# The value products of two heads, issued in turn over two PSUM banks

## The chip, the cores and the metric

One Trainium2 chip; the kernel runs on one of its cores. The metric is the device time of one execution in microseconds. TensorE is called PE (its weight loads PEld), VectorE DVE, ScalarE ACT, GpSimd POOL, and SyncE, which here only issues transfers, SP.

## What is computed

Masked attention for 8 batches of 8 heads over 576 positions with 64 values each, then a two-layer block on the 4608 tokens. Heads 0 to 3 of a batch ("plain") see the last 32 positions, heads 4 to 7 ("dilated") every fourth of the last 128.

```python
scores = np.matmul(q, k.transpose(0, 1, 3, 2)) / np.sqrt(D)
scores = np.where(masks[None], scores, -1e9)
attn = np.exp(scores - scores.max(-1, keepdims=True))
attn = attn / (attn.sum(-1, keepdims=True) + 1e-09)
x = np.matmul(attn, v).transpose(0, 2, 1, 3).reshape(B * S, H * D)
h = x @ w_in                        # (4608 x 512) @ (512 x 2048)
g = np.where(h >= 1, h, np.where(h <= -1, 0.0, (h + 1) ** 2 / 4))
return g @ w_out                    # (4608 x 2048) @ (2048 x 512)
```

## The kernel before

**Attention.** A head's 576 queries are cut into six tiles of 96, each of which sees 128 keys. The positions of dilated heads are sorted by their remainder modulo 4 on the host, so that they too have a band of keys. Heads are numbered through, n = 8 x batch + head, and are handled in pairs (n, n + 1). Scores of a head come in three parts of two tiles (`scores_split`, L230; the first 16 heads use `scores_pair`, L207). DVE adds the mask and takes the row maximum (L249, L181), ACT takes the exponential (L255), POOL divides by the sum (L291, the tile `c`), and the result is turned key by query into `pt`: by six DVE transposes (L306) for heads from 16 on, on PE (L330) with a copy out (L333) before that. Even heads use `pt0`, odd heads `pt1`.

**Values.** `values(n)` (L354) multiplies `pt` of the two heads with their values: 64 columns of weights, 96 columns moving, six tiles per head. Head n writes partitions 0 to 63, head n + 1 partitions 64 to 127 of the same PSUM tile. There are two such tiles: part 0 holds query tiles 0 to 2, part 1 tiles 3 to 5. They are called o{n}_0 and o{n}_1. Each fp32 matmul is two records in the trace, so a block has 24. `store_x` copies a tile out as a rounded part `xh` (ACT, L349) and the remainder `xl` (DVE, L350), which the first layer reads. The copies are cut where a block of 512 tokens ends (`cuts`), so a PSUM tile has one or two pieces; those of a dilated pair have two pieces each in the steady stretch, of 32 to 256 columns, since its columns are spread over the whole batch.

**PSUM.** The tag `att` has two banks, shared by the values, the scores from head 10 on, and the PE transposes of head 0 and from head 8 on. A tile that asks for a bank waits for the last reader of the tile that had it.

**The two layers.** 9 tiles of 512 tokens times 16 slices of the hidden width make 144 steps. A step has 12 matmuls of the first layer (L403, in three rounded products), the activation (DVE L417, ACT L420, DVE L422, ACT L423, DVE L426; the tiles y, h, gh, gl), and 12 matmuls of the second layer (L439) two steps later.

**Order.** PE and SP issue in the order of the code; the instructions of DVE, ACT and POOL are ordered by a scheduler that simulates the program. Attention for later batches is put into slots: slot 2s comes behind the first layer of step s, slot 2s + 1 behind its second layer. From head 16 on, for the pair n:

```python
for j, at in ((0, u), (1, u + 4)):
    place(at, lambda m=n + j: scores_split(m, 0))
    place(at + 1, lambda m=n + j: scores_split(m, 2))
    place(at + 2, lambda m=n + j: (scores_split(m, 4), after(m)))
place(u + 11, lambda n=n: values(n))
```

with u growing by 8 from pair to pair. So the slot ahead of values(n) holds the last scores of head n + 2, and the slot behind it the first scores of head n + 3, with 12 matmuls of the second layer between. The DVE transposes of head n + 2 fall behind values(n), too.

Of the kernel before, what the change touches and what calls it, by code (L numbers as in the profile page):

```python
# [22 lines left out]
F32 = mybir.dt.float32  # L23
# [9 lines left out]
QT, NQ = 96, 6  # L33
# [11 lines left out]
def body(ctx, tc, q, k, q2, k2, v, mask, eye, w_in, w_out, out):  # L45
# [5 lines left out]
    ps = ctx.enter_context(tc.tile_pool(name="ps", bufs=1, space=bass.MemoryType.PSUM))  # L51
# [269 lines left out]
    def pt_of(n):  # L321
        return first_pts[n] if n < len(first_pts) else pts[n % 2]
# [23 lines left out]
    def store_x(src, t, c, dst):  # L346
        xh, xl = xtile(t)
        with tc.high_priority(offset=60):
            last["act"] = nc.scalar.copy(out=dst(xh[:, c]), in_=src)  # L349
            last["dve"] = nc.vector.tensor_tensor(  # L350
                out=dst(xl[:, c]), in0=src, in1=dst(xh[:, c]).bitcast(F32), op=ALU.subtract
            )

    def values(n):  # L354

        b, h = divmod(n, H)
        plain = h < H // 2
        c, tok0 = h // 2, b * S

        end = TOK - tok0 % TOK  # L360
        for part in range(2):
            op = ps.tile([128, 512], F32, tag="att", name=f"o{n}_{part}", bufs=2)
            for j in range(2):
                for i in range(3):
                    PE.matmul(  # L365
                        out=op[64 * j : 64 * j + 64, i * QT : (i + 1) * QT],
                        lhsT=heads[n + j]["vt"][:, 3 * part + i],
                        rhs=pt_of(n + j)[:, 3 * part + i],
                        start=True,
                        stop=True,  # L370
                    )
            if plain:
                first = part * 3 * QT
                cuts = sorted({first, min(max(end, first), first + 3 * QT), first + 3 * QT})
                for a, z in zip(cuts, cuts[1:]):
                    t, at = divmod(tok0 + a, TOK)
                    store_x(op[:, a - first : z - first], t, c, lambda x: x[:, at : at + z - a])
            else:
                cuts = sorted({0, min(end // DIL, CLS), CLS})
                for a, z in zip(cuts, cuts[1:]):  # L380
                    t, at = divmod(tok0 + DIL * a, TOK)
                    store_x(
                        op[:, : 2 * CLS].rearrange("p (r i) -> p r i", r=2)[:, :, a:z],
                        t,
                        c,
                        lambda x: x[:, at : at + DIL * (z - a)].rearrange("p (i r) -> p r i", r=DIL)[
                            :, 2 * part : 2 * part + 2
                        ],
                    )
# [89 lines left out]
    def values_native(n):  # L479
        values(n)  # L480
        if n + 2 < native:
            load_values(n + 2)
# [8 lines left out]
    for n in range(native, nhead, 2):  # L491
        u = 27 + 4 * (n - native)
# [4 lines that stand above are left out]
        place(u + 4, lambda n=n: (transpose(n), load_values(n)))  # L497
        place(u + 8, lambda n=n: transpose(n + 1))
        place(u + 11, lambda n=n: values(n))
# [40 lines left out]
    def early_values(n):  # L540
        with tc.high_priority(offset=150):
            values(n)
# [7 lines left out]
    def marks():  # L550
        return last["act"], last["dve"]
# [5 lines left out]
    with tc.manual_schedule(engines={mybir.EngineType.PE, mybir.EngineType.SP}):  # L557
# [19 lines left out]
        first = marks()  # L577
# [110 lines left out]
```

## Time and profile before

| | |
|---|---|
| time, median of 3 runs | 943.05 us (942.95 to 943.52) |
| the profiled execution | 943.52 us, its span 941.7 us |
| granted PE clock, mean | 0.994 |
| PE busy | 924.8 us, 98% of the span |
| DVE, ACT, POOL busy | 685.0, 486.9, 239.8 us |
| values matmuls (L365) | 768 records, 24 to a block |
| steady stretch | one pair of heads every 25.13 us or so, with 24 values records |

Times of single instructions are read from a list in order of time: start, duration, engine, line, tiles (written <- read), partitions x elements, count, and in brackets how long the engine sat idle before it and what ended that. Records of PE overlap, since matmuls are pipelined: the distance of starts is what one costs. In the table of stretches, PEclk is the share of PE's clock that was granted.

### The profile page before, as it was taken

The numbers are of one execution on the slowest core, as the hardware profiler recorded it, in microseconds if no ns is written. First come the engines' busy times: TensorE is split into PE (matmuls) and PEld (weight loads), VectorE is DVE, ScalarE is ACT, GpSimd is POOL, SyncE is SP. The second block draws the span as 40 slices with busy tenths as digits, with TensorE's granted clock in tenths as the row PEclk, the third lists the DMA queues.
The fourth block names the chain that finished last, engine by engine and source line by source line (L and its number), as shares of the span: only waits on it lengthen the run. The fifth ranks groups of instructions, "written<-read, shape, count | busy, mean of one in ns | idle before, by whom it ended". The sixth has DMA issues, their size and how long they took to land.

```text
span 941.7 us, 14427 instructions
## 1 busy us (share of the span) xinstructions
PE 924.8 (98%) x4886; PEld 753.1 (80%) x4886; DVE 685.0 (73%) x1982; ACT 486.9 (52%) x1336; POOL 239.8 (25%) x155
## 2 busy tenths in 40 slices
PE   7989989999999999999999999999999999999998
PEld 6777778888888888888888888888888888888886
DVE  6898877888887888878887888888877643334333
ACT  6778856555555556555555555555555322222222
POOL 4566543222222222222222222222222000000000
PEclk9989999999999999999999999999999999999999
DMA  9971002312232222122322213222321010001001
GB/s 348 406 293 45 1 26 63 106 58 69 69 114 69 69 66 89 57 68 69 114 69 69 64 58 105 69 69 70 113 70 42 2 45 1 1 1 46 0 1 46
DMA packets 31018, 73.87 MB, mean 78 GB/s; under 512 B 3520, under 2 KB 3808, under 8 KB 30944
## 3 DMA queue, kind: packets, MB, share of 16 engines
q1 hardware_dynamic: 30944, 72.94, 23.5%
q8 instruction: 39, 0.64, 0.3%
q14 instruction: 35, 0.29, 0.1%
HBM read 63.49 MB, written 9.44 MB: 77 GB/s over the span
## 4 chain that ended last, share of the span: by engine, by line
PE 89%; DMA 5%; DVE 3%; issue 1%; POOL 1%; ACT 0%; SPq 0%; DVEq 0%; POOLq 0%; ACTq 0%
PE acc L439 41%; PE h L403 40%; PE o L365 4%; PE s L230 4%; DMA wo_raw<-w_in 3%; DMA wi_raw<-w_in 1%; DVE wo_raw L123 1%; DMA vt<-v_in 1%; DVE wo_m L126 1%; DMA kr<-k_in 1%; DVE c L181 1%; POOL c L291 0%; PE t L330 0%; DVE wi_m L126 0%; DVE y L417 0%
## 5 line engine op out<-in xcount | busy, mean ns | idle before, releaser
L439 PE MATMUL acc<-wo,gh 128*128 128x512 f32 x1152 | 385.2, 396 | 0.0
L403 PE MATMUL h<-xh,wi 128*128 128x512 f32 x1152 | 362.3, 396 | 0.8 <-DVE gl L426 0.8
L439 PEld LDWEIGHTS acc<-wo,gh 128*128 128x128 f32 x1152 | 217.0, 188 | 48.4
L403 PEld LDWEIGHTS h<-xh,wi 128*128 128x128 f32 x1152 | 210.1, 189 | 42.8 <-DVE gl L426 1.0
L403 PE MATMUL h<-xl,wi 128*128 128x512 f32 x576 | 227.5, 395 | 0.0
L439 PE MATMUL acc<-wo,gl 128*128 128x512 f32 x576 | 225.6, 392 | 0.0
L143 POOL TENSOR_TENSOR kk<-kr,kk 128x608 fp32r<-128x608 f32 x48 | 94.8, 1976 | 422.3 <-ACT kk L139 422.3
L255 ACT ACTIVATE c<-c 96x128 f32<-96x128 f32 x330 | 129.0, 392 | 118.4 <-DVE c L181 118.4
L420 ACT ACTIVATE y<-y,consts 128x512 f32<-128x512 f32 x144 | 104.1, 723 | 124.9 <-DVE y L417 124.9
L423 ACT CAST gh<-h 128x512 fp32r<-128x512 f32 x144 | 84.4, 586 | 130.4 <-PE acc L439 128.2
L417 DVE TENSOR_SCALAR y<-h 128x512 f32<-128x512 f32 x144 | 99.2, 689 | 62.9 <-PE h L403 61.7
L422 DVE TENSOR_TENSOR h<-h,y 128x512 f32<-128x512 f32 x144 | 100.6, 698 | 49.6 <-ACT y L420 48.2
L403 PEld LDWEIGHTS h<-xl,wi 128*128 128x128 f32 x576 | 108.6, 188 | 25.3
L439 PEld LDWEIGHTS acc<-wo,gl 128*128 128x128 f32 x576 | 108.6, 188 | 21.3
L426 DVE TENSOR_TENSOR gl<-h,gh 128x512 fp32r<-128x512 f32 x144 | 98.5, 684 | 37.2 <-ACT gh L423 37.2
L306 DVE STREAM_TRANSPOSE pt<-c 32x192 f32<-32x192 f32 x288 | 106.0, 368 | 5.8
L249 DVE TENSOR_TENSOR c<-s,msk 96x256 f32<-96x256 f32 (+1 forms) x168 | 61.5, 377 | 39.7 <-PE s L230 38.7
L291 POOL TENSOR_TENSOR c<-c 96x768 f32<-96x768 f32 x56 | 83.0, 1483 | 17.0 <-DVE c L290 16.7
L181 DVE CUSTOM_DVE_ANT_0 c<-s,c 96x128 f32<-96x128 f32 x288 | 70.6, 280 | 1.0
L349 ACT CAST xh<-o 128x288 fp32r<-128x288 f32 (+8 forms) x112 | 38.3, 380 | 46.2 <-PE o L365 30.8
L255 ACT ACTIVATION_READ_ACCUMULATOR c<-c 96x1 f32 x330 | 62.1, 188 | 0.0
L230 PEld LDWEIGHTS s<-kk,qs 128*96 128x96 f32 x288 | 46.4, 161 | 15.7
(57 smaller groups left out, 660.6 us busy)
## 6 DMA issues: line engine op xcount, KB each, us to landing
kr<-k_in SPq DMA_DIRECT2D x56, 304.0 KB, 3.3
qr<-q_in SPq DMA_DIRECT2D x56, 288.0 KB, 2.8
vt<-v_in SPq DMA_DIRECT2D x32, 384.0 KB, 4.0
out<-out SPq DMA_DIRECT2D x36, 256.0 KB, 2.9
wi_raw<-w_in SPq DMA_DIRECT2D x16, 512.0 KB, 9.3
wo_raw<-w_in SPq DMA_DIRECT2D x16, 512.0 KB, 9.4
msk<-mask_in SPq DMA_DIRECT2D x1, 144.0 KB, 3.8
ident<-eye_in SPq DMA_DIRECT2D x1, 36.0 KB, 4.8
```

The lines of the kernel that those rows point to most:

```text
L143: nc.gpsimd.tensor_tensor(out=kk[:, 1], in0=hd["kr"], in1=kk[:, 0].bitcast(F32), op=ALU.subtract)
L230: PE.matmul(out=sv[:, t - t0], lhsT=hd["qs"][:, t * QT : (t + 1) * QT], rhs=hd["ks"][:, :, t * QT : t * QT + 128], start=True, stop=True,)
L255: last["act"] = nc.scalar.activation(out=c[:, t], in_=c[:, t], func=AF.Exp, bias=st[:, 0, t : t + 1], scale=-1.0, accum_out=st[:, 1, t : t ...
L291: nc.gpsimd.tensor_tensor(out=c, in0=c, in1=spread(st[:, 2]), op=ALU.mult)
L306: nc.vector.transpose(out=pt[r : r + 32, :, 32 * g : 32 * g + 32], in_=c[32 * g : 32 * g + 32, :, r : r + 32],)
L403: PE.matmul(out=hp, lhsT=wi[f][:, w, 128 * c : 128 * c + 128], rhs=x[:, c], start=c == 0 and i == 0, stop=c == NC - 1 and i == len(terms) - 1,
L417: nc.vector.tensor_scalar(out=y, in0=hp, scalar1=-1.0, scalar2=1.0, op0=ALU.max, op1=ALU.min)
L420: nc.scalar.activation(out=y, in_=y, func=AF.Square, bias=half_t, scale=0.5)
L422: activated = nc.vector.tensor_tensor(out=hp, in0=hp, in1=y, op=ALU.max)
L423: copied = nc.scalar.copy(out=gh, in_=hp)
L426: nc.vector.tensor_tensor(out=gl, in0=hp, in1=gh.bitcast(F32), op=ALU.subtract)
L439: PE.matmul(out=acc[m], lhsT=g[:, r], rhs=wo[f][:, w], start=f == 0 and i == 0, stop=f == NF - 1 and i == len(terms) - 1,)
```

## The change

Both PSUM tiles of a values block are now taken at its start. The twelve matmuls alternate between the heads. In the first round head n goes through its tiles 0 to 2 into the first bank, while head n + 1 goes through its tiles 3 to 5 into the second; in the second round they swap. The copies out of both tiles follow behind all twelve matmuls, in the same code as before. No matmul, copy or size is changed, and lines behind it move down by three (L365 is L367, L417 is L420, L439 is L442).

```diff
-        for part in range(2):
-            op = ps.tile([128, 512], F32, tag="att", name=f"o{n}_{part}", bufs=2)
-            for j in range(2):
-                for i in range(3):
+        ops = [ps.tile([128, 512], F32, tag="att", name=f"o{n}_{part}", bufs=2) for part in range(2)]
+
+        for first in range(2):
+            for i in range(3):
+                for j in range(2):
+                    part = first ^ j
                     PE.matmul(
-                        out=op[64 * j : 64 * j + 64, i * QT : (i + 1) * QT],
+                        out=ops[part][64 * j : 64 * j + 64, i * QT : (i + 1) * QT],
                         lhsT=heads[n + j]["vt"][:, 3 * part + i],
                         rhs=pt_of(n + j)[:, 3 * part + i],
                         start=True,
                         stop=True,
                     )
+        for part, op in enumerate(ops):
             if plain:
```

## The prediction

> **What bounds the kernel now.** I read the page first: shares of busy time, and the chain that ended last.
>
> ```profile
> PE 924.8 (98%) x4886; PEld 753.1 (80%) x4886; DVE 685.0 (73%) x1982; ACT 486.9 (52%) x1336; POOL 239.8 (25%) x155
> PE acc L439 41%; PE h L403 40%; PE o L365 4%; PE s L230 4%; DMA wo_raw<-w_in 3%; DMA wi_raw<-w_in 1%; DVE wo_raw L123 1%; DMA vt<-v_in 1%; DVE wo_m L126 1%; DMA kr<-k_in 1%; DVE c L181 1%; POOL c L291 0%; PE t L330 0%; DVE wi_m L126 0%; DVE y L417 0%
> ```
>
> PE sets the time; the edited matmuls (L365) are 4% of the chain. Next, busy time by stage, and the groups of PE.
>
> ```profile
> 0.00:60.00 60.00, 51.94 (x440) 44.05 (x441) 48.58 (x219) 44.95 (x127) 32.99 (x28) 0.97 0.99 379
> 200.00:754.00 554.00, 554.00 (x2907) 451.43 (x2907) 448.81 (x1372) 303.56 (x910) 145.95 (x86) 1.00 0.24 72
> L230 PE MATMUL s<-kk,qs 128*96 128x256 f32 x288 | 57.7, 283 | 0.0
> ```
>
> The columns are the stage's length, then busy PE, PEld, DVE, ACT, POOL, granted clock. From 200 to 754 us PE never rests, and the scores (L230) never wait. Whatever lengthens or shortens PE's work there, or makes it wait, moves the end one for one. The first 60 us are held by DMA (0.99 busy), so the four values blocks there (n = 0 to 6) count for nothing.
>
> Then one values block in the steady stretch, n = 36, in order of time (start, duration).
>
> ```profile
> 424.27 0.40 PE L403 MATMUL h<-xl,wi 128*128 128x512 f32 x1
> 424.59 1.43 PE L365 MATMUL o<-pt,vt 128*64 128x96 f32 x24
> 425.95 0.50 PE L439 MATMUL acc<-wo,gh 128*128 128x512 f32 x1
> ...
> 428.58 0.39 PE L439 MATMUL acc<-wo,gh 128*128 128x512 f32 x1
> 428.81 0.40 PE L230 MATMUL s<-kk,qs 128*96 128x256 f32 x2
> 429.05 0.62 PE L403 MATMUL h<-xh,wi 128*128 128x512 f32 x2
> ```
>
> The block (24 records, two to a matmul) is followed by twelve L439 matmuls, and then s39_0, the first scores of head 39.
>
> **Part one: the block itself.** On PE the change puts the heads' matmuls in turn. Here pt0 is head 36, pt1 head 37; o36_0 and o36_1 are the two banks.
>
> Before, on PE at values(36):
>
> ```order
> L403 MATMUL h3_11_4389<-xl3_1952,wi11_1184 128x512
> L365 MATMUL o36_0_4410<-pt0_67,vt36_4211 64x96 x3
> L365 MATMUL o36_0_4410<-pt1_68,vt36_4211 64x96 x3
> L365 MATMUL o36_1_4421<-pt0_67,vt36_4211 64x96 x3
> L365 MATMUL o36_1_4421<-pt1_68,vt36_4211 64x96 x3
> ```
>
> After, the same place (the first eight of twelve):
>
> ```order
> L367 MATMUL o36_0_4410<-pt0_67,vt36_4211 64x96
> L367 MATMUL o36_1_4411<-pt1_68,vt36_4211 64x96
> L367 MATMUL o36_0_4410<-pt0_67,vt36_4211 64x96
> L367 MATMUL o36_1_4411<-pt1_68,vt36_4211 64x96
> L367 MATMUL o36_0_4410<-pt0_67,vt36_4211 64x96
> L367 MATMUL o36_1_4411<-pt1_68,vt36_4211 64x96
> L367 MATMUL o36_1_4411<-pt0_67,vt36_4211 64x96
> L367 MATMUL o36_0_4410<-pt1_68,vt36_4211 64x96
> ```
>
> The heads now alternate without a break, and both banks fill until the end of the block. Do heads overlap on PE? The block n = 2 tells them apart by their buffers (pts_xh, pts_xl):
>
> ```profile
> 23.34 0.71 PE L365 MATMUL o<-pts_xh,vt 128*64 128x96 f32 x6
> ...
> 24.97 0.25 PE L365 MATMUL o<-pts_xh,vt 128*64 128x96 f32 x1
> 24.99 0.25 PE L365 MATMUL o<-pts_xl,vt 128*64 128x96 f32 x1
> 25.05 0.25 PE L365 MATMUL o<-pts_xh,vt 128*64 128x96 f32 x1
> 25.07 0.25 PE L365 MATMUL o<-pts_xl,vt 128*64 128x96 f32 x1
> ```
>
> Each head starts a record every 0.08 us, the other head's between them: they run side by side already, in one and the same bank. What is lost is the lead of the first head. Six records of one head take 0.71, so the last starts 0.71 - 0.25 = 0.46 after the first; twelve would take 0.46 + 6 x 0.083 = 0.96. The block above has its last start at 1.43 - 0.25 = 1.18. If both heads start together, it saves 1.18 - 0.96 = 0.22 us. That instructions in turn do start together is seen at the scores L207, where two heads alternate over two banks:
>
> ```profile
> 109.63 1.12 PE L207 MATMUL s<-kr,qr 64*96 64x128 f32 x16
> ```
>
> Sixteen records of 128 columns in 1.12 are 0.07 each, though one alone should take 0.083 x 128/96 = 0.11: pairs run at once. The bounds are 0 (no better overlap) and 0.22; I take 0.22, since turns give overlap in both rows. The other bank itself gains nothing. The second matmul of a block now needs its bank half a block sooner; its last reader is DVE's reduce of s38_4, which stands ahead of the L140 row at 423.43 below and so is done a microsecond before the block; nothing waits.
>
> **Part two: who reads the banks, and when.** The last matmul now writes o_0, so both banks finish at the block's end, and the scheduler orders the copies out of them (L349 on ACT, L350 on DVE) anew. On DVE behind the block, before:
>
> ```order
> L417 TENSOR_SCALAR y3_11_4402<-h3_11_4389 128x512
> L350 TENSOR_TENSOR xl4_2946<-o36_0_4410,xh4_2945 128x2x64
> L422 TENSOR_TENSOR h3_11_4389<-h3_11_4389,y3_11_4402 128x512
> L350 TENSOR_TENSOR xl4_2946<-o36_1_4421,xh4_2945 128x2x64
> L350 TENSOR_TENSOR xl5_3931<-o36_0_4410,xh5_3930 128x2x80
> L306 STREAM_TRANSPOSE pt0_67<-c38_4317 32x6x32 x6
> L350 TENSOR_TENSOR xl5_3931<-o36_1_4421,xh5_3930 128x2x80
> L249 TENSOR_TENSOR c39_4444<-s39_0_4445,msk_64 96x256
> ```
>
> After:
>
> ```order
> L420 TENSOR_SCALAR y3_11_4402<-h3_11_4389 128x512
> L425 TENSOR_TENSOR h3_11_4389<-h3_11_4389,y3_11_4402 128x512
> L350 TENSOR_TENSOR xl4_2946<-o36_1_4411,xh4_2945 128x2x64
> L350 TENSOR_TENSOR xl4_2946<-o36_0_4410,xh4_2945 128x2x64
> L306 STREAM_TRANSPOSE pt0_67<-c38_4317 32x6x32 x6
> L350 TENSOR_TENSOR xl5_3938<-o36_1_4411,xh5_3937 128x2x80
> L350 TENSOR_TENSOR xl5_3938<-o36_0_4410,xh5_3937 128x2x80
> L429 TENSOR_TENSOR gl3_11_4404<-h3_11_4389,gh3_11_4403 128x512
> L249 TENSOR_TENSOR c39_4444<-s39_0_4445,msk_64 96x256
> ```
>
> Before, one bank (o36_0) was read to its end ahead of the six transposes. Now **both** second pieces stand behind them. s39_0 takes one of these banks: in the built program it waits for the second piece of o36_0 before the change, for that of o36_1 after it. All of PE's queue stands behind s39_0. The same holds for every dilated pair of the steady stretch but the last: n = 20, 22, 28, 30, 36, 38, 44, 46, 52, 54, 60, eleven in all. In plain pairs the next scores wait for a bank read out ahead of the transposes, or behind one of six.
>
> What the wait costs: DVE, ACT and POOL of before at this block.
>
> ```profile
> 423.43 0.76 DVE L140 TENSOR_TENSOR qs<-qr,qs 64x576 fp32r<-64x576 f32 x1
> ...
> 424.70 0.69 DVE L417 TENSOR_SCALAR y<-h 128x512 f32<-128x512 f32 x1
> 425.98 0.39 DVE L350 TENSOR_TENSOR xl<-o,xh 128x128 fp32r<-128x128 f32 x1 [0.59 <-ACT xh L349]
> 426.48 0.70 DVE L422 TENSOR_TENSOR h<-h,y 128x512 f32<-128x512 f32 x1
> 427.09 0.72 DVE L350 TENSOR_TENSOR xl<-o,xh 128x128 fp32r<-128x128 f32 x2
> 427.71 2.27 DVE L306 STREAM_TRANSPOSE pt<-c 32x192 f32<-32x192 f32 x6
> 430.02 0.44 DVE L350 TENSOR_TENSOR xl<-o,xh 128x160 fp32r<-128x160 f32 x1
> ```
> ```profile
> 425.56 0.39 ACT L349 CAST xh<-o 128x128 fp32r<-128x128 f32 x1 [1.11 <-PE o L365]
> 425.74 0.71 ACT L420 ACTIVATE y<-y,consts 128x512 f32<-128x512 f32 x1
> ```
> ```profile
> 425.50 1.47 POOL L291 TENSOR_TENSOR c<-c 96x768 f32<-96x768 f32 x1
> ```
>
> ACT's square y stood behind a cast; both casts now come later, so y starts when DVE's y ends, 424.70 + 0.69 + 0.04 = 425.43, and ends at 426.14. DVE's h starts at 426.17 (0.31 sooner). From h to the transposes stay two pieces and 427.71 - 426.48 = 1.23 us, so they start at 427.40; POOL's c, which they wait for, is there at 425.50 + 1.47 = 426.97. They end at 429.67, and the piece of o36_1 (0.03 + 0.44) at 430.14. From DVE to a waiting PE:
>
> ```profile
> 64.97 0.34 DVE L333 COPY pt<-t 128x192 f32<-128x192 f32 x1
> ```
> ```profile
> 65.37 1.43 PE L365 MATMUL o<-pt,vt 128*64 128x96 f32 x24 [1.79 <-DVE pt L333]
> ```
>
> that is 65.37 - 65.31 = 0.06. So s39_0 starts at 430.20. PE gets there at 428.81 - 0.22 = 428.59 and waits 1.61; against before it is 430.20 - 428.81 = 1.39 late. The other pairs divide 288 columns differently into first and second pieces. Two copies from DVE's rows price a column:
>
> ```profile
> 106.86 0.58 DVE L350 TENSOR_TENSOR xl<-o,xh 128x224 fp32r<-128x224 f32 x1 [0.76 <-ACT xh L349]
> ...
> 109.20 0.27 DVE L350 TENSOR_TENSOR xl<-o,xh 128x64 fp32r<-128x64 f32 x1 [0.16 <-ACT xh L349]
> ```
>
> 0.31 for 160 columns, 0.002 each. Two first pieces and a second stand before the release: 416 columns at n = 36, 480 at n = 20, 320 at n = 60, 407 on average. So the delay runs from 1.2 to 1.5 us, 1.37 in the mean. The next wait, s39_2 on the other piece (one copy later, about 430.6), finds PE 2.8 us further on: free.
>
> **The sum.** Of the 28 blocks behind the first 60 us, eleven are late by 1.37: +15.1. Seventeen save 0.22: -3.7. Together +11.4 on the profiled execution, 943.52 us (its span is 941.7), which is the highest of three runs around 943.05: 954.9, or 954.4 from the median. I say 954.8. Lower bound of the wait: transposes at once behind POOL, 427.03, 0.37 sooner, gives 4.1 less, 950.7.
>
> **Rivals.** *The clock drops in the waits.* Two stretches of before in which PE waits, each with the stretch behind it:
>
> ```profile
> 12.21:15.62 3.41, 2.28 (x34) 1.84 (x32) 3.04 (x29) 3.41 (x19) 3.07 (x3) 1.00 1.05 411
> 15.62:19.03 3.41, 2.84 (x30) 2.52 (x26) 2.74 (x25) 2.79 (x9) 3.41 (x3) 1.00 1.02 393
> ```
> ```profile
> 42.93:46.34 3.41, 2.02 (x17) 1.62 (x17) 3.41 (x21) 3.08 (x11) 2.45 (x2) 1.00 1.02 405
> 46.34:49.75 3.41, 3.41 (x19) 3.41 (x18) 3.41 (x13) 3.41 (x8) 1.47 (x1) 0.50 1.03 411
> ```
>
> Behind 2.28 of 3.41 us busy (34 records) the clock stayed whole; behind 2.02 (17 short records) the next 3.41 us were granted 0.50. A wait of 1.6 leaves 1.8 to 1.9 us busy, by that measure under both, but of unbroken 128x512 matmuls; so the rows leave it open. It must also lie wholly in one such stretch, which happens for (3.41 - 1.6)/3.41 = 0.53. Each would cost 3.41/2 = 1.7. All eleven: 0.53 x 11 x 1.7 = 9.9, so 965; the six longest alone 5.4, so 960. The Trainium skill (TensorE: Matmul & The Clock Gate, Part 1) lets the clock fall after a whole idle window of about 3.4 us; by that no wait here would do it, but the row at 42.93, well over half busy, disagrees.
>
> *No better overlap.* The lead of the first head stays, plain pairs save nothing, and the eleven are as late: 943.5 + 15.1 = 958.6. Against it stand the two rows on overlap. The Trainium skill (TensorE: Matmul & The Clock Gate, Part 3) says that a weight load overlaps running matmuls only where the row group differs; both heads use all 128 rows, so by that rule turns would gain nothing. The rows of n = 2 disagree.
>
> *Faster.* The release comes before PE does, by 428.59, and all 28 blocks save 0.22: 943.5 - 6.2 = 937.3. It needs the transposes 1.6 us sooner, at 425.8, ahead of POOL's 426.97; or a bank other than the built program names. That bounds it.
>
> **Chances.** Forecast 0.46; clock drops too 0.34; no better overlap 0.08; faster 0.08; a wait mostly swallowed, within a few us of no change, 0.04. A measurement here tells 0.2% (1.9 us) from no change. The range reaches from 948 (below the lower bound of the wait) to 966 (all waits lose clock); the faster case stays out. Faster 0.08, same 0.03, slower 0.89.
>
> **What would show it.** A values block of 24 records with its last start at 0.96 instead of 1.18; an idle of about 1.6 us before the L230 scores of eleven pairs, put down to DVE xl L350; none at plain pairs; DVE's transposes at the same length, 2.27. I am wrong if L230 shows no idle time, or if the block keeps 1.18, and too low if the clock row falls to 0.50 in the steady stretch.

## The result, and the profile after

The change takes the kernel from 943.0 us (median of four runs, 942.9 to 943.52) to 959.22 us (958.53 to 960.58): ratio 1.0171, 95% interval 1.0156 to 1.0187. The profiled execution took 959.26 us, its span 957.5.

First the page of the changed kernel: busy time by engine, the chain that ended last, and the scores' group.

```profile
PE 920.7 (96%) x4886; PEld 744.8 (78%) x4886; DVE 684.8 (72%) x1982; ACT 488.6 (51%) x1336; POOL 240.0 (25%) x155
...
PE 83%; DVE 8%; DMA 5%; ACT 2%; issue 1%; POOL 0%; SPq 0%; DVEq 0%; ACTq 0%
PE h L406 39%; PE acc L442 37%; PE s L230 4%; DMA wo_raw<-w_in 3%; DVE pt L306 2%; PE o L367 2%; DVE xl L350 1%; DVE y L420 1%; DMA wi_raw<-w_in 1%; ACT y L423 1%; DVE h L425 1%; DVE wo_m L126 1%; DMA kr<-k_in 1%; DVE wi_m L126 0%; DMA msk<-mask_in 0%
...
L230 PE MATMUL s<-kk,qs 128*96 128x256 f32 x288 | 58.2, 284 | 16.2 <-DVE xl L350 16.2
```

PE is busy 4 us less, and the span is 16 us longer. L230, which never waited before, has 16.2 us of idle time, all put down to the copies L350. DVE's transposes (L306) and copies (L350) now stand on the chain; they did not before.

The waits of PE by who ended them (total, times, longest):

```profile
PE s L230 <- DVE xl L350: 16.2, 11, 1.6
PE s L207 <- DVE c L181: 2.9, 6, 0.8
PE h L406 <- DVE gl L429: 2.1, 2, 1.1
PE o L367 <- DVE pts_xh L333: 1.8, 2, 1.2
...
PE o L367 <- DVE xl L350: 1.6, 2, 1.2
PE t L330 <- DVE xl L350: 1.4, 2, 1.2
```

Eleven waits before the scores, one behind each of the dilated pairs that the forecast names. The waits of L367 for pts_xh and for xl belong to the first 60 us; they come up again below.

The block n = 36 and what follows on PE, then DVE and ACT, in order of time:

```profile
431.98 1.21 PE L367 MATMUL o<-pt,vt 128*64 128x96 f32 x24
433.12 0.50 PE L442 MATMUL acc<-wo,gh 128*128 128x512 f32 x1
...
435.75 0.39 PE L442 MATMUL acc<-wo,gh 128*128 128x512 f32 x1
437.63 0.45 PE L230 MATMUL s<-kk,qs 128*96 128x256 f32 x2 [1.49 <-DVE xl L350]
437.91 0.62 PE L406 MATMUL h<-xh,wi 128*128 128x512 f32 x2
```
```profile
432.08 0.69 DVE L420 TENSOR_SCALAR y<-h 128x512 f32<-128x512 f32 x1
433.56 0.70 DVE L425 TENSOR_TENSOR h<-h,y 128x512 f32<-128x512 f32 x1 [0.79 <-ACT y L423]
434.17 0.66 DVE L350 TENSOR_TENSOR xl<-o,xh 128x128 fp32r<-128x128 f32 x2
434.74 2.27 DVE L306 STREAM_TRANSPOSE pt<-c 32x192 f32<-32x192 f32 x6
437.04 0.78 DVE L350 TENSOR_TENSOR xl<-o,xh 128x160 fp32r<-128x160 f32 x2
```
```profile
432.81 0.72 ACT L423 ACTIVATE y<-y,consts 128x512 f32<-128x512 f32 x1 [0.97 <-DVE y L420]
433.44 0.60 ACT L349 CAST xh<-o 128x128 fp32r<-128x128 f32 x2
```

The 24 records of the block take 1.21 us instead of 1.43: the last start is 0.96 after the first, 0.22 sooner. On DVE the second pieces, both of them, come behind 2.27 us of transposes. The first of the two is done at 437.48 (in the row they are merged), and the scores start at 437.63, 1.88 after the last L442 instead of the 0.23 of before: 1.65 us of waiting. The pair takes 26.61 us from this block to the next, where 25.13 were taken before.

### The profile page after: what moved, and what is told of

Its sections match the earlier page's. It is cut to its first block, busy times and chain, and to the rows that moved or that the text cites. A ratio compares the mean times of both kernels' runs of the same rounds, so it can differ in the third digit from the quotient of the medians.

```text
span 957.5 us, 14419 instructions
## 1 busy us (share of the span) xinstructions
PE 920.7 (96%) x4886; PEld 744.8 (78%) x4886; DVE 684.8 (72%) x1982; ACT 488.6 (51%) x1336; POOL 240.0 (25%) x155
## 4 chain that ended last, share of the span: by engine, by line
PE 83%; DVE 8%; DMA 5%; ACT 2%; issue 1%; POOL 0%; SPq 0%; DVEq 0%; ACTq 0%
PE h L406 39%; PE acc L442 37%; PE s L230 4%; DMA wo_raw<-w_in 3%; DVE pt L306 2%; PE o L367 2%; DVE xl L350 1%; DVE y L420 1%; DMA wi_raw<-w_in 1%; ACT y L423 1%; DVE h L425 1%; DVE wo_m L126 1%; DMA kr<-k_in 1%; DVE wi_m L126 0%; DMA msk<-mask_in 0%
## 5 line engine op out<-in xcount | busy, mean ns | idle before, releaser
L442 PE MATMUL acc<-wo,gh 128*128 128x512 f32 x1152 | 385.4, 396 | 0.0
L406 PE MATMUL h<-xh,wi 128*128 128x512 f32 x1152 | 361.9, 395 | 2.1 <-DVE gl L429 2.1
L442 PEld LDWEIGHTS acc<-wo,gh 128*128 128x128 f32 x1152 | 217.0, 188 | 48.6
L406 PEld LDWEIGHTS h<-xh,wi 128*128 128x128 f32 x1152 | 209.7, 189 | 44.3 <-DVE gl L429 2.5
L406 PE MATMUL h<-xl,wi 128*128 128x512 f32 x576 | 227.6, 395 | 0.0
L442 PE MATMUL acc<-wo,gl 128*128 128x512 f32 x576 | 225.6, 392 | 0.0
L420 DVE TENSOR_SCALAR y<-h 128x512 f32<-128x512 f32 x144 | 99.2, 689 | 76.5 <-PE h L406 75.5
L406 PEld LDWEIGHTS h<-xl,wi 128*128 128x128 f32 x576 | 108.4, 188 | 25.4
L442 PEld LDWEIGHTS acc<-wo,gl 128*128 128x128 f32 x576 | 108.6, 189 | 21.1
L306 DVE STREAM_TRANSPOSE pt<-c 32x192 f32<-32x192 f32 x288 | 106.0, 368 | 5.8
L230 PE MATMUL s<-kk,qs 128*96 128x256 f32 x288 | 58.2, 284 | 16.2 <-DVE xl L350 16.2
L230 PEld LDWEIGHTS s<-kk,qs 128*96 128x96 f32 x288 | 45.6, 161 | 35.0 <-issue 20.5
```

Source lines behind the costliest of these rows:

```text
L230: PE.matmul(out=sv[:, t - t0], lhsT=hd["qs"][:, t * QT : (t + 1) * QT], rhs=hd["ks"][:, :, t * QT : t * QT + 128], start=True, stop=True,)
L306: nc.vector.transpose(out=pt[r : r + 32, :, 32 * g : 32 * g + 32], in_=c[32 * g : 32 * g + 32, :, r : r + 32],)
L406: PE.matmul(out=hp, lhsT=wi[f][:, w, 128 * c : 128 * c + 128], rhs=x[:, c], start=c == 0 and i == 0, stop=c == NC - 1 and i == len(terms) - 1,
L420: nc.vector.tensor_scalar(out=y, in0=hp, scalar1=-1.0, scalar2=1.0, op0=ALU.max, op1=ALU.min)
L442: PE.matmul(out=acc[m], lhsT=g[:, r], rhs=wo[f][:, w], start=f == 0 and i == 0, stop=f == NF - 1 and i == len(terms) - 1,)
```

## Experiments

Theory: (a) turns shorten every block by 0.22 us, whatever the bank; (b) eleven waits come from both banks ending late, so that both last copies fall behind the transposes; (c) the first four blocks, which the forecast took for free, cost some 3 us. The rivals of each run stand in its expectation. Ratios are against the kernel before, timed on the same chip.

| run | median us | ratio, 95% interval |
|---|---|---|
| change from n = 8 on | 956.20 | 1.0141 (1.0124 to 1.0158) |
| change for n = 0 to 6 | 946.57 | 1.0041 (1.0026 to 1.0057) |
| turns in one bank | 937.97 | 0.9948 (0.9935 to 0.9962) |
| change, copies ahead of transposes | 941.34 | 0.9981 (0.9971 to 0.9990) |
| change for n = 0, 2 | 945.10 | 1.0018 (1.0009 to 1.0026) |
| change for n = 6 | 944.46 | 1.0012 (1.0004 to 1.0021) |
| head by head, two banks | 967.63 | 1.0256 (1.0240 to 1.0271) |
| turns in one bank, from n = 8 on | 938.01 | 0.9940 (0.9928 to 0.9953) |
| from n = 8 on, copies ahead | 937.70 | 0.9936 (0.9923 to 0.9950) |
| change for plain pairs from n = 8 on | 940.46 | 0.9972 (0.9961 to 0.9982) |

**Late blocks or early ones.** The change is applied by a condition on n (n < H in the other run, H being 8); where it is false, the loops of before stand. An excerpt:

```diff
+        turns = n >= H
+        order = [(0, j, i) for j in range(2) for i in range(3)] + [(1, j, i) for j in range(2) for i in range(3)]
+        if turns:
+            order = [(f ^ j, j, i) for f in range(2) for i in range(3) for j in range(2)]
...
```

From n = 8 on:

> The change for the 28 pairs from n = 8 on; the first four blocks (n = 0 to 6) as before. Theory (the eleven waits before the scores cost 15.6 us against before, the shorter blocks of the other pairs give 3 to 4 back, and the first four blocks cost the 3 us that the forecast lacked): 955.5 to 956.5 us, with the eleven waits on DVE xl L350 still 16 us in sum. Rival (the first blocks are free behind the transfers, and the forecast's shortfall lies in the waits): 959, as the whole change.

956.20, with the same 16.2 us of idle time before L230. For n = 0 to 6:

> The change for n = 0 to 6 alone; all later blocks as before. Theory (the second matmul of an early block now waits for the copy that comes last, and later work starts later): 945.4 to 946.6 us, values block n = 8 some 3 us later than before, no wait before the L230 scores. Rival (transfers set the pace of the first 60 us): 943.0, block n = 8 where it was.

946.57, some 3 us over before. So the two halves of the loss are apart: about 13 us from the waits less what shorter blocks give, about 3 from the first four blocks. The rival that the transfers hide those blocks is out.

How much of the 3 us is the waits themselves is less clear. The six runs for n = 0 to 6 go with their mean granted clock: 944.65 at 0.998, 945.39 at 0.996, 946.48 and 946.66 at 0.994, 947.81 at 0.992 and 948.57 at 0.993. And in the profile of the whole change the clock falls to half in two stretches of the first 60 us:

```profile
22.05:25.47 3.42, 3.42 (x26) 2.78 (x22) 2.75 (x6) 2.78 (x7) 3.20 (x3) 0.50 1.03 407
39.12:42.53 3.41, 3.41 (x14) 2.38 (x15) 2.61 (x6) 3.19 (x8) 0.44 (x1) 0.50 1.02 407
```

The first begins behind the waits in block 0, the second behind the wait in block 6. The kernel before has two such stretches as well, but at other places (46.34, in the prediction, and 66.82, below).

**One bank instead of two.** Heads still take turns, but a bank is finished before the other is begun (against the kernel before).

```diff
         for part in range(2):
             op = ps.tile([128, 512], F32, tag="att", name=f"o{n}_{part}", bufs=2)
-            for j in range(2):
-                for i in range(3):
+            for i in range(3):
+                for j in range(2):
```

> Heads in turn, but both in the same bank: part 0 is finished first, then part 1, as before the change. Theory (turns shorten a block to 0.96 between first and last start whatever the bank, and the waits come from both banks ending late): blocks of 0.96, L230 without idle time, 28 x 0.22 = 6 us less than before, 936.5 to 938. Rival one (two heads in turn need two banks): blocks stay at 1.18 or grow, 943 or more. Rival two (the waits come from the turns, not from the second bank): idle time of some 16 us before L230, 953 or more.

937.97, 5.2 us less than its runs of before. The values block and the scores' group of this run:

```profile
422.65 1.21 PE L365 MATMUL o<-pt,vt 128*64 128x96 f32 x24
```
```profile
L230 PE MATMUL s<-kk,qs 128*96 128x256 f32 x288 | 57.7, 283 | 0.0
```

The block is as short as in the change (1.21), and nothing waits. Turns are worth their 0.22 us in one bank; the second bank adds only the waits. Both rivals are out.

**The copies ahead of the transposes.** The whole change; the six transposes are ordered behind the copies of the bank that was stored last. The start of the edit, against the changed kernel:

```diff
         c = heads[n]["c"]
-        for g in range(3):
+        with tc.issue_after(last["dve"].ins):
+            for g in range(3):
...
```

> The whole change, and the six DVE transposes of a head are ordered on DVE behind the copies of the last bank that was stored. Theory (the eleven waits are the transposes standing ahead of a bank's last copy): idle time before L230 gone, 938.5 to 941.5 us, that is 6 less than before for the blocks and some 3 more for the first four. Rival (DVE is simply late, whatever the order, or the later transposes make the next values block wait): L230 or L367 idle for 10 us or more, 950 or more.

941.34. PE's order is that of the change; on DVE at n = 36 (start, duration):

```profile
428.23 0.66 DVE L351 TENSOR_TENSOR xl<-o,xh 128x128 fp32r<-128x128 f32 x2
429.12 0.45 DVE L351 TENSOR_TENSOR xl<-o,xh 128x160 fp32r<-128x160 f32 x1 [0.23 <-ACT xh L350]
429.47 0.74 DVE L307 STREAM_TRANSPOSE pt<-c 32x192 f32<-32x192 f32 x2
430.24 0.45 DVE L351 TENSOR_TENSOR xl<-o,xh 128x160 fp32r<-128x160 f32 x1
430.71 1.52 DVE L307 STREAM_TRANSPOSE pt<-c 32x192 f32<-32x192 f32 x4
```
```profile
L230 PE MATMUL s<-kk,qs 128*96 128x256 f32 x288 | 57.7, 282 | 0.0
```

The first second piece now comes ahead of the transposes, the 16.2 us of idle time before L230 are gone, and the time falls by 18 us. The same work in another order on DVE: the wait was the order and not the load.

**Which of the first blocks.** The condition is n < 4 in one run, n == 6 in the other.

> Turns over two banks for n = 0 and 2 alone, everything else as before. Theory (the 3 us of the first four blocks come from second matmuls that wait; block 0 waits for the copy of head 1's last transposes, and its delay is handed on): about half of them, 944 to 945.5 us, block n = 6 some 1.5 us later than before, n = 8 likewise. Rival (only the wait inside block 6 counts, the earlier blocks are hidden behind the transfers): 943.0 to 943.5.

945.10, 1.6 us over its runs of before (943.55), in the expected range. But block 6 came 2.6 us later than before, counted from block 0 (17.75 against 15.15), and not 1.5; in its profile the clock is at 0.50 from 23.00 to 29.82, twice as long as in the changed kernel.

Block 0 and the PE transposes behind it, in the kernel before:

```profile
19.12 1.18 PE L365 MATMUL o<-pts_xh,vt 128*64 128x96 f32 x12
20.60 0.71 PE L365 MATMUL o<-pts_xh,vt 128*64 128x96 f32 x8 [0.29 <-DVE pts_xh L333]
21.72 0.55 PE L365 MATMUL o<-pts_xh,vt 128*64 128x96 f32 x4 [0.41 <-DVE pts_xh L333]
22.20 1.21 PE L330 MATMUL t<-ident,c 96*128 96x96 f32 x12
```

In the changed kernel, with the two DVE copies that it waits for:

```profile
18.94 0.38 PE L367 MATMUL o<-pts_xh,vt 128*64 128x96 f32 x2
20.51 0.39 PE L367 MATMUL o<-pts_xh,vt 128*64 128x96 f32 x4 [1.19 <-DVE pts_xh L333]
21.54 1.41 PE L367 MATMUL o<-pts_xh,vt 128*64 128x96 f32 x18 [0.65 <-DVE pts_xh L333]
22.88 2.18 PE L330 MATMUL t<-ident,c 96*128 96x96 f32 x12
```
```profile
20.02 0.34 DVE L333 COPY pts_xh<-t 128x192 f32<-128x192 f32 x1
21.14 0.34 DVE L333 COPY pts_xh<-t 128x192 f32<-128x192 f32 x1
```

By the code, the second matmul opens the second bank, which held the PE transposes of head 0's tiles 4 and 5 until the first of these copies was done; the fourth matmul reads head 1's tiles 4 and 5, which the second copy brings. Before, twelve of the 24 records ran ahead of the first wait in this block and four after the last; now two do, and 18 run after the last. The twelve transposes behind the block take 2.18 instead of 1.21, in the stretch of half clock. So of the 1.84 us by which block 2 starts later after block 0 (6.06 against 4.22), about half stands in these transposes.

> Turns over two banks for n = 6 alone. Theory (its second matmul waits for the last copy out of block 4, which stands on DVE behind a weight step): a wait of 1.2 to 1.5 us inside block 6, block n = 8 some 1.5 us later, 944 to 945.5 us. Rival (only blocks 0 and 2 count): 943.0 to 943.5, n = 8 where it was.

944.46, 0.9 us over, near the lower end; but not as expected. In its profile block 8 starts 1.4 us sooner after block 0 than before (44.89 against 46.25), not later, and block 6 is only 0.40 longer than the 1.21 without a wait. First this run, then the changed kernel:

```profile
33.64 1.61 PE L371 MATMUL o<-pt,vt 128*64 128x96 f32 x24
```
```profile
36.25 0.35 PE L367 MATMUL o<-pt,vt 128*64 128x96 f32 x2 [0.46 <-issue]
37.83 1.18 PE L367 MATMUL o<-pt,vt 128*64 128x96 f32 x22 [1.23 <-DVE xl L350]
```

So that wait needs the changed blocks before it as well (0, 2 and 4), and why block 6 alone costs 0.9 us is not settled: the stretches of half clock lie elsewhere in this profile too (from 72.38 and 130.41 on).

**Two banks without turns.** All of head n first, then head n + 1 (against the changed kernel).

```diff
-        for first in range(2):
-            for i in range(3):
-                for j in range(2):
-                    part = first ^ j
+        for j in range(2):
+            for part in range(2):
+                for i in range(3):
```

> All twelve matmuls in the order head n first (both banks), then head n + 1: no turns at all, yet both banks end at the end of the block, as in the change. Theory (the eleven waits come from both banks ending late, not from turns; and the lead of the first head is the point at which its third-last record starts, 0.22 us with six records, 0.22 + 6 x 0.083 = 0.72 with twelve): last start 0.72 + 0.96 = 1.68 after the first, eleven waits before L230 of 13 to 16 us in sum, 966 to 971 us. Rival one (PE looks over the whole block, so the lead is fixed): last start 1.18 or less. Rival two (turns make the waits): no idle time before L230, 950 to 957.

967.63, in the range. Block and scores:

```profile
384.42 1.92 PE L366 MATMUL o<-pt,vt 128*64 128x96 f32 x24
```
```profile
L230 PE MATMUL s<-kk,qs 128*96 128x256 f32 x288 | 58.2, 284 | 8.5 <-DVE xl L350 8.5
```

The last start is 1.92 - 0.25 = 1.67 after the first (1.68 expected). Eleven waits appear without any turns, so they come from both banks ending late and not from the turns. Their sum was expected wrongly: PE arrives 1.67 - 0.96 = 0.71 later than in the change, which makes each wait that much shorter, 16.2 - 11 x 0.71 = 8.4; measured 8.5.

**The best parts together.** Turns in one bank, but only from n = 8 on (the condition n < H keeps the old order of the two inner loops):

> Turns in one bank at a time for n from 8 on, the first four blocks as before. Theory (28 shorter blocks, no new wait anywhere): 28 x 0.22 = 6.1 less than before at most, 937 us. If the first blocks were worth something in the run with turns everywhere: 938 or more here against that run; if they cost something there: 936.5 to 937.5.

938.01. The interval (0.9928 to 0.9953) holds the full 6.1 us and cannot be told from turns everywhere (0.9948): with one bank, the first blocks are worth nothing either way that shows. And two banks from n = 8 on with the copies ahead of the transposes:

> Turns over two banks from n = 8 on, the first four blocks as before, and the six DVE transposes of a head ordered behind the copies. Theory (without the eleven waits and without the first four blocks nothing of the change is left but the shorter blocks, so two banks are as good as one): the time of the runs with turns in one bank, 937 to 938.5. Rival (something else in taking both banks at once costs): 940 or more.

937.70, no idle time before L230. Without the waits and the first four blocks, two banks are as good as one and no better. All three versions, at 0.9936 to 0.9948, beat both kernels.

**Plain pairs alone.** The condition is n >= H and plain.

> Turns over two banks for the 14 plain pairs from n = 8 on alone; dilated pairs and the first four blocks as before. Theory (plain pairs release a bank ahead of the transposes): no idle time before L230, 14 x 0.22 = 3.0 us less than before, 940 to 940.8 us. Rival (any pair whose both banks end late makes the next scores wait): idle time before L230, 943 or more.

940.46, 2.9 us less than its runs of before (943.34); 14 x 0.22 is 3.1. And the scores:

```profile
L230 PE MATMUL s<-kk,qs 128*96 128x256 f32 x288 | 57.7, 283 | 0.0
```

Both banks end late here too, yet nothing waits. A plain pair's bank without a cut is copied in one piece of 288 columns, in this trace always ahead of the six transposes or, as at n = 18, behind one of them:

```profile
200.07 0.37 DVE L306 STREAM_TRANSPOSE pt<-c 32x192 f32<-32x192 f32 x1
200.37 0.41 DVE L350 TENSOR_TENSOR xl<-o,xh 128x288 fp32r<-128x288 f32 x1
...
```

That copy is done at 200.78, and the next scores start at 201.67. So banks that end late make a wait only where the last copies of both stand behind the transposes.

## Why the prediction was right, point by point

- **What bounds the kernel.** Right for the steady stretch: there a pair with a wait takes 1.31 to 1.60 us more than before, and one without takes 0.21 less.
- **The block.** 1.18 to 0.96 was forecast; 1.21 - 0.25 = 0.96 was measured, in one bank and in two.
- **The second bank gains nothing, and its earlier need costs nothing in the steady stretch.** Right (937.97 with one bank; 937.70 with two).
- **The wait.** Its place, the number of waits and their cause were right. Its working held link by link at n = 36: square y right behind DVE's y, h 1.48 us behind the start of y (forecast 1.47), transposes 1.18 behind h (1.23). The term was a little small: a pair is longer by 1.60 us at n = 20 down to 1.31 at n = 60, where 1.5 and 1.2 stood. The periods of the eleven pairs sum to 16.2 us more than before; 15.1 was forecast. At n = 36 the difference is in two handovers: from the end of the copy (437.48) to the scores 0.15 pass where 0.06 was taken, and from the first scores to L406 0.28 (437.63 to 437.91) where 0.24 stood (428.81 to 429.05).
- **"The first four blocks count for nothing".** This step failed. It was read from the share of DMA in the first 60 us, and a full DMA does not mean that PE's order is covered. The question that was missed there is what each matmul waits for, its bank and its tiles, and in what order the copies that release them are made; the waits inside blocks 0 and 2 stood in the trace of before. The changed blocks 0 to 6 cost 3.4 us by their own run (946.57 against 943.17). How much of that is waits and how much half clock behind them stays open.
- **The sum.** Eleven pairs +16.2, seventeen blocks -3.6 (0.21 each), first blocks +3.1 (the rest of 959.26 - 943.52 = 15.7). Forecast +15.1, -3.7 and 0. The point was 4.4 us low: about three quarters from the one step, the rest from the size of the wait.
- **The clock rival.** It did not happen in the eleven waits. Busy time by stretch in the changed kernel:

```profile
200.60:766.50 565.90, 549.69 (x2899) 444.19 (x2898) 446.40 (x1369) 304.10 (x906) 147.60 (x87) 1.00 0.24 71
332.67:336.08 3.41, 1.87 (x10) 1.38 (x9) 3.31 (x12) 0.66 (x2) 0.00 (x0) 1.00 0.15 59
336.08:339.49 3.41, 3.41 (x18) 2.78 (x17) 1.70 (x10) 1.72 (x6) 0.00 (x0) 1.00 0.00 0
```

The granted clock stays 1.00 over all eleven waits and in the 5 us behind each of them, also behind a stretch that holds one whole wait and is busy for 1.87 of 3.41 us. Half clock came elsewhere, in three stretches (from 22.05, 39.12 and 131.28 on), as many as before (46.34, 66.82 and 128.26). The measured time lies near the price of this rival (960 to 965), and nearer still to that of no better overlap (958.6), by chance alone: the block of 0.96 rules the second out.

## What to carry to other kernels

Before two accumulators are opened at once, ask when each is read out and who asks for its bank next: an in-order copy engine may put long work between the end of the block and the last copy, and one early release is what hides that. Independent halves of PE's columns run side by side when their instructions alternate, in one bank as in two, so take the turns and leave the release where it was. A stage in which DMA is full still has an order on PE: waits moved to the head of the first blocks cost some 3 us here, with the half clock behind them.

## What the runs showed of the hardware

- Two heads on different column halves of PE, both with all 128 rows, run side by side, also while they write one bank: each head starts a record every 0.08 us, as in a run of one head alone. Without turns the second head begins when three records of the first are left to start: last starts of 0.96, 1.18 and 1.67 us after the first, with turns, runs of six records and runs of twelve.
- Recorded busy time alone does not tell when the clock drops. The same piece of work, the block n = 8 behind a wait of 1.79 us, and the stretch behind it, first in the kernel before, then in the changed one:

```profile
63.41:66.82 3.41, 1.62 (x26) 1.33 (x25) 3.41 (x4) 1.62 (x3) 1.76 (x2) 1.00 0.80 323
66.82:70.23 3.41, 3.41 (x8) 2.66 (x9) 2.73 (x6) 3.15 (x7) 1.36 (x1) 0.50 0.41 115
```
```profile
66.43:69.84 3.41, 1.62 (x26) 1.20 (x25) 3.41 (x4) 1.62 (x3) 2.10 (x2) 1.00 0.88 357
69.84:73.25 3.41, 3.23 (x18) 2.24 (x13) 2.58 (x5) 2.81 (x7) 1.36 (x1) 1.00 0.37 120
```

Both are busy for 1.62 us with 26 records. Behind the first the clock fell to 0.50, behind the second it did not, and what decides between them stays open.
